# A longer first and a shorter second filler of matmuls at the start of a fused attention and MLP kernel

## The chip, the cores and the metric

The kernel runs on one core of a Trainium2 chip. The metric is device time of one execution in microseconds (us). "Span" is the time from the first to the last instruction in the trace. It is about 1.7 us shorter than the device time here. Every execution has a device time and a span, but only one execution of each kernel and label left a full trace.

Time before the change: 265.46 us, the median of three executions (265.42 to 265.71).

## The reference, cut to what matters

```python
# x: 1 x 2048 x 640, bf16
g = sigmoid((x * gate_w).sum(-1))          # gate per token
a = linear_attention(x, wqkv) @ wo         # 32 heads of 20; phi(t) = where(t>0, t+1, exp(t)) + 1e-6
b = mixer_and_mlp(x, w1, w2, w3, w4)       # layernorm, gelu, shifted groups, residual, MLP
out = g * a + (1 - g) * b
```

The argument is about the first eight microseconds, in which x tiles 0 to 3 (128 tokens each) are loaded, transposed on TensorE, and multiplied by the q part of `wqkv`.

## The kernel before

A small scheduler in the kernel's Python orders all work and adds the semaphore waits. The order of TensorE's start is this (cuts marked):

```python
sch.dma("act", junk[...], A_wqkv[...], "touch")
dma_in(x_tok[:, 0:2, :], x2[0:256, :]..., "x01")      # x tiles 0 and 1
load_wq(0)
dma_in(x_tok[:, 2:4, :], x2[256:512, :]..., "x23")    # x tiles 2 and 3
for k in range(1, KD):
    load_wq(k)
...
memset(pool, ones_c[:], 1.0)                          # 128 x 768, the fillers' operand
...
NWARM = 5
NWARM2 = 2

def t_x(t):                                           # transpose x tile t on TensorE
    b = bank()
    tr_group(b, [x_tok[:, t, 128 * k:128 * (k + 1)] for k in range(KD)])
    ...
    if t % 2:
        activation(dst, src, ACTF.Copy)               # odd tiles: ScalarE copies PSUM to xT
    else:
        copy(dve, dst, src)                           # even tiles: VectorE
...
def warmup(n, cyc):
    b = bank()

    def fn(e):
        ins = None
        for _ in range(n):
            ins = e.matmul(ps[:, b, :], ones_c[:, 0:128], ones_c[:, 128:640], start=True, stop=True)
        return ins
    pe(fn, [ones_c[:, 0:640]], [ps[:, b, :]], cost=n * cyc)
...
def q_four():
    order = [(0, 0), (1, 0), (2, None), (3, None), (0, 1), (1, 1), (2, 0), ...]   # (tile, k); None: transpose the tile
    stream(order, wq, 128, lambda t, b: phi(b, pq_tok[:, t, :]))
...
addA(("warm",), 0.0, lambda: warmup(NWARM, 427.0))    # first filler
for i in range(2):
    addA(("tx", i), 0.28, lambda i=i: t_x(i))         # transposes of x tiles 0 and 1
addA(("warm", 1), 0.0, lambda: warmup(NWARM2, 300.0)) # second filler
addA(("q", 3), 5.44, q_four)
```

The fillers' results are never read. They exist only to keep TensorE active while nothing real can run.

Of the kernel before, what the change touches and what calls it, by code (L numbers as in the profile page):

```python
# [424 lines left out]
def _build(nc, A_x, A_wqkv, A_wo, B_w1, B_w2, B_w3, B_w4, gate_w, out, dbg=None, stop=None):  # L425
# [42 lines left out]
    ps = nc.alloc_psum_tensor("ps", [128, 8, 512], F32)  # L468
# [5 lines left out]
    ones_c = pa.alloc("ones_c", [128, 768], BF16)  # L474
# [45 lines left out]
    def bank():  # L520
        best = None
        for k_ in range(nbanks[0]):
            b = (bank_rr[0] + k_) % nbanks[0]
            if b in bank_pend or b in bank_hold:
                continue
            lk = sch.locks.get(b)
            tfree = 0.0 if lk is None else sch.ev_time.get((lk[1].sem, lk[1].val), 1e18)
            if best is None or tfree < best[0]:
                best = (tfree, b)
        bank_rr[0] = best[1] + 1  # L530
        bank_pend.add(best[1])
        return best[1]
# [58 lines left out]
    def pe(fn, reads, writes, cost=500.0):  # L591
        for w_ in writes:
            sp_, rl = sch.rects(w_)
            if sp_ == "ps":
                for (_p0, _p1, lo, hi) in rl:
                    for b in range(lo // PS_BANK, (hi - 1) // PS_BANK + 1):
                        bank_pend.discard(b)
        return sch.op("pe", fn, reads, writes, cost=cost)
# [141 lines left out]
        assert tags.get((buf, sl)) == what, ("stale ring slot", buf, sl, what, tags.get((buf, sl)))  # L740

    IT = _Items()
    NWARM = 5
    NWARM2 = 2

    def t_x(t):
        b = bank()
        tr_group(b, [x_tok[:, t, 128 * k:128 * (k + 1)] for k in range(KD)])
        src = psb(b, 0, D).rearrange("p (k c) -> p k c", k=KD)
        dst = xT[:, :, 128 * t:128 * (t + 1)]  # L750
        if t % 2:
            activation(dst, src, ACTF.Copy)
        else:
            copy(dve, dst, src)
# [70 lines left out]
        tag_chk("xn", sx, (which, t))  # L825
        sch.dma("sp", xnT[:, :, 128 * t:128 * (t + 1)], xn[:, sx, :], "trn%d" % slot("trn", 4), transpose=True)

    def warmup(n, cyc):
        b = bank()

        def fn(e):
            ins = None
            for _ in range(n):
                ins = e.matmul(ps[:, b, :], ones_c[:, 0:128], ones_c[:, 128:640], start=True, stop=True)  # L834
            return ins
        pe(fn, [ones_c[:, 0:640]], [ps[:, b, :]], cost=n * cyc)

    def q_tile(t):
        tok = slice(128 * t, 128 * (t + 1))
# [37 lines left out]
    def addA(name, dur, fn, deps=()):  # L877
        IT.add("A", name, dur, fn, deps)

    addA(("warm",), 0.0, lambda: warmup(NWARM, 427.0))  # L880
    for i in range(2):
        addA(("tx", i), 0.28, lambda i=i: t_x(i))
    addA(("warm", 1), 0.0, lambda: warmup(NWARM2, 300.0))
    addA(("q", 3), 5.44, q_four)
    addA(("k", 0), 1.36, k_first)
    for i in range(1, 4):
# [324 lines left out]
def bass_gated_mix__linear_attn_block__mixer_s_mlp__prompt_kernel(  # L1211
    nc, A_x, A_wqkv, A_wo, B_x, B_w1, B_w2, B_w3, B_w4, gate_w, out
):
    assert tuple(A_x.shape) == (1, S, D) and tuple(out.shape) == (1, S, D)
    assert tuple(A_wqkv.shape) == (D, 3 * D) and tuple(A_wo.shape) == (D, D)
    assert tuple(B_w1.shape) == (D, D) and tuple(B_w2.shape) == (D, D)
    assert tuple(B_w3.shape) == (D, F) and tuple(B_w4.shape) == (F, D) and tuple(gate_w.shape) == (D,)
    _build(nc, A_x, A_wqkv, A_wo, B_w1, B_w2, B_w3, B_w4, gate_w, out)
# [28 lines left out]
```

## Time and profile before

| what | value |
|---|---|
| device time, median of 3 | 265.46 us |
| span of the profiled execution (its own device time was 266.33 us) | 264.6 us |
| TensorE (PE) busy | 258.2 us, 98% |
| PE's share of the chain that ended last | 96% |

The head of the page, and the first line of its chain, of the kernel before:

```profile
span 264.6 us, 4264 instructions
PE 258.2 (98%) x1675; PEld 136.4 (52%) x1707; DVE 145.9 (55%) x242; ACT 107.6 (41%) x216; POOL 91.1 (34%) x148
...
PE 96%; DMA 1%; issue 1%; ACT 0%; DVE 0%
```

PE is TensorE, PEld its weight loads, DVE VectorE, ACT ScalarE and POOL GpSimd. TensorE bounds the kernel. A saving at its start should therefore reach the end. The next fence is PE's timeline of the kernel before. The columns are start (us), time from the start of the first to the end of the last instruction of the row (us), engine, line, operation, output and inputs, and a count. In brackets stands the idle time in front and what ended it.

```profile
start us, us, engine line op out<-in xcount [idle before <-releaser]
1.59 2.32 PE L834 MATMUL ps<-ones_c 128*128 128x512 bf16 x5 [1.59 <-POOL ones_c L665]
4.12 1.25 PE L617 MATMUL ps<-ident,x_tok 128*128 128x128 bf16 x10 [0.21 <-DMA x_tok<-in_A_x_dram]
5.16 1.06 PE L834 MATMUL ps<-ones_c 128*128 128x512 bf16 x2
6.01 0.63 PE L858 MATMUL ps<-wq,xT 128*128 128x512 bf16 x1
6.44 0.31 PE L859 MATMUL ps<-wq,xT 128*128 128x128 bf16 x1
...
7.08 1.02 PE L617 MATMUL ps<-ident,x_tok 128*128 128x128 bf16 x10
7.93 0.38 PE L858 MATMUL ps<-wq,xT 128*128 128x512 bf16 x1
```

Read the distances between starts, not the durations, because a duration (0.63 us at 6.01) runs on past the start of the next matmul (6.44). At 6.01 to 6.44 us a 512-column matmul takes 0.43 us. Later in the trace it takes 0.22 us. The first fillers stream until about 1.59 + 5 x 0.427 = 3.73 us. The transposes begin at 4.12 us, so nothing streams for about 0.39 us (the page counts 0.21 us, since the duration that it gives the last filler ends later).

The row at 7.93 us is the first q step after the second group of transposes, and it is called **the first pair**.

### The profile page before, as it was taken

Reading aid. Unit: us, or ns where it says so; the run is one execution under the profiler, and the core shown is the slowest. Engines: PE = TensorE matmul, PEld = TensorE weight load, DVE = VectorE, ACT = ScalarE, POOL = GpSimd, SP = SyncE. Lnnn points to the kernel's source line nnn. Section 1 sums busy time; section 2 is a strip of 40 time slices with the busy share of each in tenths; the row PEclk is TensorE's granted clock in tenths of the full one; section 3 lists DMA queues with packets and bytes.
Section 4 is the critical chain, followed back from the end, with each engine's and each line's share of the span. In section 5 each row is a group of like instructions: output and inputs, shape, how many; then the busy total and the mean of one; then the engine's idle time right before and its main releaser. Section 6 shows DMA issues by size and latency. Waiting matters only on the chain.

```text
span 264.6 us, 4264 instructions
## 1 busy us (share of the span) xinstructions
PE 258.2 (98%) x1675; PEld 136.4 (52%) x1707; DVE 145.9 (55%) x242; ACT 107.6 (41%) x216; POOL 91.1 (34%) x148
## 2 busy tenths in 40 slices
PE   7999999999999999999999999999999999999996
PEld 3655555555555454554444545554545455545553
DVE  0397877899903797999786886312212121122242
ACT  3486767742365758675661031212211222121000
POOL 4003996849774017487821104001110011021020
DMA  6775898551666895253666731120000200002011
GB/s 203 244 103 147 205 146 149 162 115 24 102 121 104 299 373 82 54 99 60 69 124 124 110 68 25 33 93 0 2 0 0 102 0 0 2 0 99 2 50 50
DMA packets 50595, 24.77 MB, mean 94 GB/s; under 512 B 41996, under 2 KB 49165, under 8 KB 50576
## 3 DMA queue, kind: packets, MB, share of 16 engines
q1 hardware_dynamic: 49328, 21.23, 36.3%
q0 software_dynamic: 1152, 3.28, 5.4%
q8 instruction: 13, 0.21, 0.3%
q14 instruction: 6, 0.05, 0.1%
q10 hardware_dynamic: 96, 0.00, 0.0%
HBM read 12.05 MB, written 2.62 MB: 55 GB/s over the span
## 4 chain that ended last, share of the span: by engine, by line
PE 96%; DMA 1%; issue 1%; ACT 0%; DVE 0%
PE ps L606 60%; PE ps L1103 21%; PE ps L786 8%; PE ps L858 2%; DMA x_tok<-in_A_x_dram 1%; PE ps L1085 1%; PE ps L1025 1%; PE ps L617 1%; PE ps L859 1%; PE ps L944 1%; DVE x_tok L645 0%; PE ps L834 0%; ACT h2T L662 0%; ACT M_sb L662 0%
## 5 line engine op out<-in xcount | busy, mean ns | idle before, releaser
L662 ACT ACTIVATE h2T<-ps 128x512 bf16<-128x512 f32 x52 | 31.0, 597 | 86.5 <-PE ps L606 86.5
L606 PE MATMUL ps<-xnT,w_58 128*128 128x512 bf16 x250 | 59.0, 379 | 0.5
L1103 PE MATMUL ps<-w_84,h2T 128*128 128x128 bf16 (+1 forms) x412 | 58.2, 298 | 0.4 <-issue 0.3
L628 POOL TENSOR_SCALAR abx<-x_tok,stg 128x640 f32<-128x640 bf16 x16 | 13.9, 874 | 107.6 <-DVE x_tok L645 71.0
L1103 PEld LDWEIGHTS ps<-w_84,h2T 128*128 128x128 bf16 x416 | 32.4, 98 | 27.8 <-issue 2.1
L645 DVE SCALAR_TENSOR_TENSOR x_tok<-ps,stg,abx 128x640 bf16<-128x640 f32 (+2 forms) x17 | 14.3, 844 | 50.7 <-PE ps L1103 50.7
L606 PEld LDWEIGHTS ps<-xnT,w_58 128*128 128x128 bf16 x260 | 24.3, 98 | 24.9 <-issue 0.4
L645 DVE SCALAR_TENSOR_TENSOR abx<-ps,stg,abx 128x640 f32<-128x640 f32 x16 | 14.1, 882 | 28.5 <-PE ps L606 25.5
L662 ACT ACTIVATE Er<-ps 128x640 bf16<-128x640 f32 x32 | 22.4, 704 | 12.7 <-PE ps L606 8.5
L662 ACT ACTIVATE hsT<-ps 128x512 bf16<-128x512 f32 (+1 forms) x32 | 18.9, 593 | 14.6 <-PE ps L606 14.3
L661 ACT ACTIVATE junk<-x_tok 128x640 bf16<-128x640 bf16 x32 | 23.6, 736 | 2.0 <-DVE x_tok L643 1.7
L606 PE MATMUL ps<-M_sb,pqnT 128*128 128x128 bf16 (+1 forms) x157 | 23.7, 298 | 0.2
L606 PE MATMUL ps<-w_60,hsT 128*128 128x128 bf16 (+1 forms) x158 | 23.6, 298 | 0.1
L786 PE MATMUL ps<-pk_tok,x_tok 128*128 128x128 bf16 (+1 forms) x156 | 23.3, 297 | 0.2
L606 PE MATMUL ps<-xnT,w_59 128*128 128x512 bf16 x96 | 23.2, 379 | 0.3 <-issue 0.2
L606 PE MATMUL ps<-wkg,xT 128*128 128x131 bf16 (+1 forms) x148 | 22.4, 298 | 0.1
L606 PEld LDWEIGHTS ps<-M_sb,pqnT 128*128 128x128 bf16 x160 | 13.3, 98 | 12.4 <-issue 0.4
L606 PEld LDWEIGHTS ps<-w_60,hsT 128*128 128x128 bf16 x160 | 13.3, 98 | 12.2
L628 POOL TENSOR_SCALAR xn<-x_tok,st_54 128x640 bf16<-128x640 bf16 x16 | 17.4, 1090 | 4.7 <-DMA xnT<-xn 4.6
L606 PE MATMUL ps<-wq,xT 128*128 128x128 bf16 (+1 forms) x118 | 18.2, 298 | 0.1
L628 POOL TENSOR_SCALAR xn<-x_tok,st_55 128x640 bf16<-128x640 bf16 x16 | 16.3, 1028 | 3.6 <-DMA xnT<-xn 3.2
L628 DVE TENSOR_SCALAR Er<-Er 128x640 bf16<-128x640 bf16 x32 | 12.0, 375 | 9.4 <-ACT Er L662 9.2
(74 smaller groups left out, 264.2 us busy)
## 6 DMA issues: line engine op xcount, KB each, us to landing
w_58<-in_B_w_dram SPq DMA_DIRECT2D x1, 2160.0 KB, 8.2
w_84<-in_B_w_dram SPq DMA_DIRECT2D x1, 2080.0 KB, 13.6
x_tok<-in_A_x_dram SPq DMA_DIRECT2D x3, 640.0 KB, 5.5
out_dram<-x_tok SPq DMA_DIRECT2D x3, 640.0 KB, 3.3
wq<-in_A_wqkv_dram SPq DMA_DIRECT2D x5, 160.0 KB, 4.4
wkg<-in_A_wqkv_dram SPq DMA_DIRECT2D x5, 160.0 KB, 4.4
wv<-in_A_wqkv_dram POOLq DMA_DIRECT2D x1, 800.0 KB, 6.3
wo_aug<-in_A_wo_dram POOLq DMA_DIRECT2D x5, 150.0 KB, 5.1
```

The source lines that it names most:

```text
L606: ins = e.matmul(out_ap, l, r, start=(i == 0), stop=(i == n - 1))
L617: ins = e.transpose(o, s_, ident[:])
L628: return engf(lambda e: e.tensor_scalar(out_ap, in_ap, s1, s2, op0, op1), rd, [out_ap], cost=cost)
L645: return dve(lambda e: e.scalar_tensor_tensor(out_ap, in0, scalar, in1, op0, op1), rd, [out_ap], cost=cost)
L661: return act(lambda e: e.activation(out_ap, in_ap, func, bias=bias, scale=scale, accum_out=accum), rd, wr, cost=cost)
L662: return act(lambda e: e.activation(out_ap, in_ap, func, bias=bias, scale=scale), rd, wr, cost=cost)
L786: ins = e.matmul(o, l, r, start=(t0 + q_ == 0), stop=(t0 + q_ == NT - 1))
L858: e.matmul(ps[:, b, 0:512], l, w[:, k, 0:512], start=(k == 0), stop=(k == KD - 1))
L859: return e.matmul(ps[:, b + 1, 0:n2], l, w[:, k, 512:512 + n2], start=(k == 0), stop=(k == KD - 1))
L944: ins = e.matmul(o, l, r_, start=st_, stop=sp_, skip_group_check=True)
L1025: ins = e.matmul(o, l, r, start=st, stop=sp)
L1103: ins = e.matmul(o, l, r, start=False, stop=(i == KFF - 1))
```

## The change

The intent is that TensorE be busy without a break from its first instruction until x tiles 0 and 1 land, so that its clock rises earlier. The first filler goes from 5 x 512 to 6 x 512 columns. The second goes from 2 x 512 to 512 + 2 x 128.

```diff
-    NWARM = 5
-    NWARM2 = 2
+    WARM = 3072
+    WARM2 = 768
...
-    def warmup(n, cyc):
+    def warmup(cols, cyc):
         b = bank()
+        steps = [512] * (cols // 512) + [128] * (cols % 512 // 128)
 
         def fn(e):
             ins = None
-            for _ in range(n):
-                ins = e.matmul(ps[:, b, :], ones_c[:, 0:128], ones_c[:, 128:640], start=True, stop=True)
+            for n in steps:
+                ins = e.matmul(ps[:, b, 0:n], ones_c[:, 0:128], ones_c[:, 128:128 + n], start=True, stop=True)
             return ins
-        pe(fn, [ones_c[:, 0:640]], [ps[:, b, :]], cost=n * cyc)
+        pe(fn, [ones_c[:, 0:640]], [ps[:, b, :]], cost=cols * cyc)
...
-    addA(("warm",), 0.0, lambda: warmup(NWARM, 427.0))
+    addA(("warm",), 0.0, lambda: warmup(WARM, 0.834))
...
-    addA(("warm", 1), 0.0, lambda: warmup(NWARM2, 300.0))
+    addA(("warm", 1), 0.0, lambda: warmup(WARM2, 0.42))
```

## The prediction

> **What bounds the kernel now.** TensorE. The page has PE busy 258.2 of 264.6 us (98%), and the chain of waits that ended last is PE for 96% of the span, DMA for 1% and issue for 1%. After 8 us the view of waits shows no single PE wait over 0.2 us. So a microsecond saved on TensorE at the start should reach the end, unless a later load or VectorE/ScalarE has too little slack.
>
> **What happens at the start (timeline of PE).** The five 512-column fillers begin at 1.59 us, 0.43 us apart, so their streaming is over near 3.73. The transposes of x tiles 0 and 1 begin at 4.12, when the x load issued at 0.80 us has landed (3.27 us in the chain). That leaves about 0.39 us without streaming. Everything up to 7.08 us is slow: 512-column matmuls 427 ns apart, transposes 107 ns apart; from 7.93 us on a 512 plus 128 pair takes 0.27 us, half. The ten transposes from 7.08 to 7.93 fit some six slow and four fast ones, so the clock rises at about 7.7 us: 3.6 us after the break, 6.1 us after the first matmul. The profile's granted clock reads 1.00 throughout, so only the spacing shows this. [...]
>
> **What the change does.** It adds a sixth 512 filler: streaming then ends near 1.59 + 6 x 0.427 = 4.15 us, so the transposes start at most 0.03 us later. The second filler shrinks from 1024 to 768 columns: 0.64 us slow or 0.33 fast instead of 0.85. No other work is added or moved; the emission order should stay nearly the same, since most scheduling dependences shift with TensorE.
>
> **Costing.** [...] transposes to about 5.2, filler to 5.6, first q step to 5.85. The second q step then waits for ScalarE's copy of tile 1 (0.70 us, about 5.4 to 6.1): a new PE idle near 0.3 us. It ends near 6.4, when x tiles 2 and 3 land (issued 1.82 us, 4.6 us to landing), so their transposes run about 6.4 to 6.95 instead of ending at 7.93. The wq slices (issued from 2.3 us on, about 4.5 us each) land just before use. Gain: 0.95 us. If the clock still rises at 7.7 us, only the shorter filler counts: 0.2 - 0.03 = about 0.15 us. Nearly all of either lies on the critical path. I weigh the first case more[...].
>
> **Predicted:** 264.7 us (0.3% faster), range 264.2 to 265.5. Chances: faster by over 2% 0.01, within 2% 0.98, slower by over 2% 0.01.
>
> **What would show it right.** PE timeline: six fillers, no gap before the transposes at about 4.15; spacing halved near 5.1 us rather than 7.7; the first pair after the second transposes near 7.0 instead of 7.93; a short idle before the second q step released by ScalarE's copy; everything after it shifted by the same 0.9 us, and the same idle total later.
>
> **What would make it wrong.** [...] X tiles 2 and 3 or a wq slice may land too late to be used sooner, so that PE waits for DMA instead. A different instruction order later, or a fixed-time load, may take the shift back.

The costing began from a rise of the clock near 5.1 us, an assumption, and its times from "transposes to about 5.2" on hold for that rise. The sum came to a gain of 0.95 us with this rise and of about 0.15 us with the rise still at 7.7 us. Weighed together they gave 264.7 us, 0.76 us under the 265.46.

## The result, and the profile after

In the first set of runs the changed kernel took 265.70 us, the median of 6 executions (264.97 to 266.20). The kernel before took 265.65 us in the same rounds (265.42 to 266.42). The ratio is 0.9994, with a 95% interval of 0.9974 to 1.0015: the same. A ratio here is the mean time of one kernel's fast executions over that of the other's of the same rounds, so it is not quite the ratio of the medians.

The two profiled executions look quite different from that verdict. The head of the page, its chain, and PE's timeline of the changed kernel:

```profile
span 263.2 us, 4300 instructions
PE 259.0 (98%) x1709; PEld 135.5 (51%) x1709; DVE 145.4 (55%) x242; ACT 107.7 (41%) x216; POOL 91.0 (35%) x148
...
PE 98%; DVE 0%; POOL 0%; issue 0%; POOLq 0%
```

```profile
1.58 2.74 PE L835 MATMUL ps<-ones_c 128*128 128x512 bf16 x6 [1.58 <-POOL ones_c L665]
4.17 0.76 PE L617 MATMUL ps<-ident,x_tok 128*128 128x128 bf16 x10
4.77 0.49 PE L835 MATMUL ps<-ones_c 128*128 128x512 bf16 x3
5.33 0.38 PE L859 MATMUL ps<-wq,xT 128*128 128x512 bf16 x1
5.54 0.22 PE L860 MATMUL ps<-wq,xT 128*128 128x128 bf16 x1
...
6.01 0.72 PE L617 MATMUL ps<-ident,x_tok 128*128 128x128 bf16 x10
6.57 0.38 PE L859 MATMUL ps<-wq,xT 128*128 128x512 bf16 x1
```

The ten transposes from 4.17 us take 0.60 us to the next row instead of 1.04. The clock has risen by then, and the first pair stands at 6.57 us instead of 7.93, so 1.36 us earlier. All of that arrives at the end. These are the last rows of VectorE's timeline, first of the kernel before, then of the changed one:

```profile
261.32 1.08 DVE L645 SCALAR_TENSOR_TENSOR x_tok<-ps,stg,abx 128x512 bf16<-128x512 f32 x2 [1.92 <-PE ps L1103]
```

```profile
259.96 1.07 DVE L645 SCALAR_TENSOR_TENSOR x_tok<-ps,stg,abx 128x512 bf16<-128x512 f32 x2 [1.92 <-PE ps L1104]
```

The difference is 1.36 us again. The order of instructions on every engine is the same in both traces, apart from the fillers (for TensorE by its weight loads, as some matmul records are missing). So one pair of profiles says "1.36 us faster", and the executions say "no difference". The explanation is in the executions. The six spans of the changed kernel are 263.2, 263.5, 263.8, 264.1, 264.2 and 264.5 us. The profile caught the fastest of them. The profiled execution of the kernel before (266.33 us) was slower than all three timed ones that came with it (265.42 to 265.71). A single profile of each was a draw from two wide distributions that overlap.

The trace's record of the granted clock says what is drawn. It holds only changes of the clock: a start, a duration, and the granted share. For the changed kernel's profiled execution it reads as follows (ns; the span starts at 10414 and ends at 273650 on the same scale):

```
start 14680   duration 259413   share 1.0
start 274093  duration 1603     share 0.5
```

The clock rose at 14680 - 10414 = 4266 ns, so at 4.27 us of the span. It stayed up for 259413 ns. A later trace shows one other duration (256000 ns, with three fillers); the two differ by 3413 ns. Every rise below is read from this record, unless it is said to come from the spacing. The kernel before has no record in its trace, so its rise was read from the spacing: about 7.7 us. The page's granted clock reads 1.00 in both, though the 512-column matmuls before the rise stood 0.43 us apart and those after it 0.22 us. It can't be used for the start.

### The profile page after: what moved, and what is told of

Read it like the earlier page. It is cut to its first block, busy times and chain, and to the rows that moved or that the text cites. A ratio compares the mean times of both kernels' runs of the same rounds, so it can differ in the third digit from the quotient of the medians.

```text
span 263.2 us, 4300 instructions
## 1 busy us (share of the span) xinstructions
PE 259.0 (98%) x1709; PEld 135.5 (51%) x1709; DVE 145.4 (55%) x242; ACT 107.7 (41%) x216; POOL 91.0 (35%) x148
## 4 chain that ended last, share of the span: by engine, by line
PE 98%; DVE 0%; POOL 0%; issue 0%; POOLq 0%
PE ps L606 61%; PE ps L1104 22%; PE ps L786 8%; PE ps L859 2%; PE ps L835 1%; PE ps L1086 1%; PE ps L1026 1%; PE ps L945 1%; PE ps L860 1%; PE ps L617 0%; DVE x_tok L645 0%; POOL ones_c L665 0%; POOLq L1233 0%
## 5 line engine op out<-in xcount | busy, mean ns | idle before, releaser
L606 PE MATMUL ps<-xnT,w 128*128 128x512 bf16 x360 | 84.3, 379 | 0.0
L1104 PE MATMUL ps<-w,h2T 128*128 128x512 bf16 (+1 forms) x416 | 58.7, 299 | 0.0
L606 PEld LDWEIGHTS ps<-xnT,w 128*128 128x128 bf16 x360 | 33.5, 98 | 33.5 <-issue 0.4
L1104 PEld LDWEIGHTS ps<-w,h2T 128*128 128x128 bf16 x416 | 32.4, 98 | 27.8 <-issue 2.1
L628 POOL TENSOR_SCALAR xn<-x_tok,st 128x640 bf16<-128x640 bf16 x32 | 33.5, 1056 | 12.2 <-DMA xnT<-xn 11.8
L606 PE MATMUL ps<-M_sb,pqnT 128*128 128x512 bf16 (+1 forms) x160 | 23.9, 299 | 0.0
L786 PE MATMUL ps<-pk_tok,x_tok 128*128 128x512 bf16 (+1 forms) x160 | 23.9, 299 | 0.0
L606 PE MATMUL ps<-w,hsT 128*128 128x512 bf16 (+1 forms) x160 | 23.7, 299 | 0.0
L606 PE MATMUL ps<-wkg,xT 128*128 128x512 bf16 (+1 forms) x150 | 22.6, 299 | 0.0
L606 PE MATMUL ps<-wq,xT 128*128 128x512 bf16 (+1 forms) x120 | 18.3, 299 | 0.0
```

The costliest lines, as they stand in the source:

```text
L606: ins = e.matmul(out_ap, l, r, start=(i == 0), stop=(i == n - 1))
L628: return engf(lambda e: e.tensor_scalar(out_ap, in_ap, s1, s2, op0, op1), rd, [out_ap], cost=cost)
L786: ins = e.matmul(o, l, r, start=(t0 + q_ == 0), stop=(t0 + q_ == NT - 1))
L1104: ins = e.matmul(o, l, r, start=False, stop=(i == KFF - 1))
```

## The experiments

Two theories were put side by side after the first result.

- **W (a sum).** What counts is how long TensorE streamed in all in the last microseconds before the rise. A break costs only its own length from the sum. When the rise comes differs between executions.
- **U (unbroken work).** The clock rises about 3.6 us after unbroken work began, as it did in the first profile of the kernel before (4.12 to 7.7 us), and the break of 0.39 us sets the count back to zero. This is what the prediction had built on.

Both are conjectures. The ranges of the rise that the expectations give under W are estimates. The earliest rise is the first matmul plus about 2.5 us of streaming, plus the break where there is one (1.58 + 2.5 = 4.1 us for the changed kernel, 4.4 to 4.5 us for the kernel before). With three first fillers or none it is the start of the transposes at 4.12 us plus 2.5 us, so 6.6 us. The 2.5 us lie between 2.31 us, streamed in the kernel before from 1.59 to about 4.29 us without a rise there, and 2.66 us, streamed in the changed kernel from 1.58 us to the rise at 4.27 us. The latest rise is put 3.4 us after the earliest, the size of the 3413 ns above; that this bounds it was not shown.

Four sets of runs were made, each on one chip, with the kernel before run 11 times in each set. Below, "mean" is the mean of one kernel's executions in us.

### The two kernels again, unchanged

The first two runs of set one had no edit.

> The changed kernel again, unchanged. Theory W [...]: the rise falls anywhere from about 4.1 to 7.5 us, so this profile will show another rise than the 4.2 us of the first, and the spans of its executions spread over about 1.2 us or more. Rival U [...]: this profile shows the rise near 5 us or earlier like the first one, and spans agree within 0.3 us. Rival N (the spread comes from somewhere after 20 us, not from the start): the first pair after the second transposes stands at the same time as in the first profile (6.57 us), and the span differs all the same.

Measured: the rise came at 6.55 us and the first pair at 7.29 us. The mean was 265.64 (265.07 to 266.98), and the ratio to the kernel before was 0.9982 (0.9960 to 1.0005). PE's timeline:

```profile
1.58 2.74 PE L835 MATMUL ps<-ones_c 128*128 128x512 bf16 x6 [1.58 <-POOL ones_c L665]
4.15 1.25 PE L617 MATMUL ps<-ident,x_tok 128*128 128x128 bf16 x10
...
7.29 0.38 PE L859 MATMUL ps<-wq,xT 128*128 128x512 bf16 x1
```

> The kernel before again, unchanged. W: the rise falls anywhere from about 4.4 to 7.8 us, most likely earlier than the 7.7 us of the first profile, and the first pair after the second transposes correspondingly earlier than 7.93, by half the difference of the rises. U: the rise is again at 7.5 to 7.8 us and the pair at 7.93. Mean of its spans: as the changed kernel plus 0.1 to 0.3 us by W; plus about 1.3 us by U.

Measured: the rise came at 4.87 us and the first pair at 6.97 us. The mean was 265.79, ratio 0.9991 (0.9973 to 1.0009) to the other executions of the very same kernel. PE's timeline of this copy of the kernel before:

```profile
1.58 2.31 PE L834 MATMUL ps<-ones_c 128*128 128x512 bf16 x5 [1.58 <-POOL ones_c L665]
4.14 1.06 PE L617 MATMUL ps<-ident,x_tok 128*128 128x128 bf16 x10 [0.24 <-DMA x_tok<-in_A_x_dram]
5.04 0.59 PE L834 MATMUL ps<-ones_c 128*128 128x512 bf16 x2
5.53 0.38 PE L858 MATMUL ps<-wq,xT 128*128 128x512 bf16 x1
...
6.97 0.38 PE L858 MATMUL ps<-wq,xT 128*128 128x512 bf16 x1
```

This is the decisive reading against U. The same code, with the same break before 4.14 us, has its clock up 0.73 us after the break. The copy of the changed kernel, with no break, has it up only at 6.55 us. In this pair of profiles the old kernel is the faster one, by 0.32 us at the first pair. The kernel with the earlier rise is the faster one in both pairs, whichever code it runs. The rival N of the expectation (the spread comes from later) falls too. The time from the first pair to the end was 256.66 or 256.67 us in all four of these profiles.

### Fewer first fillers

```diff
-    NWARM = 5
+    NWARM = 3
```

> Three first fillers instead of five in the kernel before: the break before the first transposes grows from 0.39 to about 1.25 us, nothing else moves. W: [...] the rise comes at 6.6 to 10.0 us, on average 2.2 us later than before, and the time grows by about 1.1 us (266.7 us, ratio 1.004). U, and any rule by which the break of 0.39 us already spoils the count: same rise and same time as before, within 0.1%.

Measured: the rise came at 8.36 us. The mean was 266.72, ratio 1.0023 (1.0002 to 1.0044). The break is now an idle of 1.13 us on the page:

```profile
1.58 1.46 PE L834 MATMUL ps<-ones_c 128*128 128x512 bf16 x3 [1.58 <-POOL ones_c L665]
4.17 1.25 PE L617 MATMUL ps<-ident,x_tok 128*128 128x128 bf16 x10 [1.13 <-DMA x_tok<-in_A_x_dram]
...
8.20 0.46 PE L858 MATMUL ps<-wq,xT 128*128 128x512 bf16 x1
```

The direction is W's. U's "same within 0.1%" is not excluded by this run: the interval begins at 1.0002. The size was too large in my expectation: 0.6 us in its own rounds instead of 1.1. I had taken half a microsecond of time for each microsecond of rise. The profiles give less: 4.27 to 6.57 and 6.55 to 7.29 in the changed kernel, so 0.72 / 2.28 = 0.32 us per us. A faster clock is partly spent on waiting at the start, for example 0.27 us for the load of x tiles 2 and 3 in the run without a second filler below. The expected shift of 2.2 us of rise is then worth 0.7 us, an estimate that fits the 0.6 us.

```diff
-    addA(("warm",), 0.0, lambda: warmup(NWARM, 427.0))
+    # first filler left out
```

> No first filler at all in the kernel before. W: [...] the rise comes at 6.6 to 10.0 us as with three fillers: time equal to that run within 0.2%, about 1 us (0.4%) over the kernel before. U: same time as before within 0.1%. A third view, that any filler before the break helps in proportion to its length, would put this run slower than the one with three fillers by as much again as that one is slower than before.

Measured: rise 7.15 us, mean 266.80, ratio 1.0026 (1.0010 to 1.0042). This looks like a hit for W, but the run was flawed. PE waited 0.34 us for ScalarE's copy of x tile 3, which neither theory foresaw. Printing the bank choices of the kernel's Python showed the cause. Leaving the filler out also leaves out its PSUM bank (the kernel deals out eight of them for TensorE's results). All later banks shift, and q tile 2 gets bank 0, from which ScalarE is still copying x tile 3; in the kernel before it gets banks 2 and 3, and tile 3 has bank 1. The same flaw is in the run without a second filler below. This run was therefore repeated with the bank still taken:

```diff
-    addA(("warm",), 0.0, lambda: warmup(NWARM, 427.0))
+    addA(("warm",), 0.0, lambda: bank_pend.discard(bank()))
```

> No first filler in the kernel before, as in the earlier run without one, but its PSUM bank is still taken, so that every later bank is chosen as in the kernel before. The earlier run had moved q tile 2 onto the bank that ScalarE was still copying tile 3 from, a wait of 0.34 us (0.5 us of streaming) that the filler as such does not cause. Now: no such wait, 256.7 us from the first pair after the second transposes to the end if the clock is up by then. W [...]: rise 6.6 to 10.0 us and the time of the run with three fillers, 266.7 us, within 0.25 us; 0.7 us or more over the kernel before. View that the fillers help in proportion to their length: clearly slower than with three. View that the break of 0.39 us spoils the count anyway: as the kernel before.

Measured: five executions of 266.41 to 267.39, mean 266.86, ratio 1.0033 (1.0014 to 1.0052). One further execution took 703.61 us; it is set aside here (see the last section), but it is the one that was traced, so this kernel's rise and the absence of the wait were not seen. Within its noise no first filler costs the same as three, both 0.6 to 0.9 us over the kernel before, while the step from three to five gains all of it. W had expected the same time for both. A gain in proportion to filler length would put no filler at about 1.5 us (2.5 x 0.6, an estimate). The interval here (0.4 to 1.4 us) leaves that just outside, but the one of three fillers is too wide (0.1 to 1.2 us) for the times alone to exclude it. The view that five fillers with a break are already spoilt is excluded, since leaving them out would then cost nothing, and it cost 0.4 to 1.4 us.

### The two halves of the change, alone

```diff
-    WARM2 = 768
+    WARM2 = 1024
```

> The first filler of six matmuls alone; the second filler stays at 1024 columns as before. W [...]: the rise is drawn from the same range as in the changed kernel, about 4.1 to 7.5 us, 0.4 us earlier than before on average; four profiles so far give about 0.33 us of time for one us of rise, so about 0.13 us (0.05%) is gained on the kernel before, inside the noise of 0.2%. At a given rise the first pair after the second transposes stands where it does in the kernel before (line through 4.87, 6.97 and 7.7, 7.93). U (unbroken work needed) is already against the runs; it would give 0.9 us or more.

Measured: rise 4.65 us, mean 265.75, ratio 1.0001 (0.9984 to 1.0019). The timeline of this run shows two things:

```profile
1.58 2.74 PE L835 MATMUL ps<-ones_c 128*128 128x512 bf16 x6 [1.58 <-POOL ones_c L665]
4.49 0.79 PE L617 MATMUL ps<-ident,x_tok 128*128 128x128 bf16 x10 [0.16 <-DMA x_tok<-in_A_x_dram]
...
6.91 0.38 PE L859 MATMUL ps<-wq,xT 128*128 128x512 bf16 x1
```

First, x landed late, so even six fillers left a break. Streaming stopped near 1.58 + 6 x 0.427 = 4.14 us, 0.35 us before the transposes. The aim of the change, no break until x lands, depends on a landing time that moves by 0.3 us between executions (transposes from 4.15 us in the first copy of the changed kernel, from 4.49 us here). Second, the clock rose 0.16 us after that break. U can't produce this. The expected line for the first pair (6.90 us at a rise of 4.65) was met with 6.91.

This execution did not keep its early start. A later wait for a transposing DMA took 0.5 us of it back, as the waits of PE in the same run show (columns: who waited, for whom, total us, times, longest us):

```profile
PE ps L606 <- DMA xT<-x_tok: 0.3, 1, 0.3
```

It stands at 42.28 us in the chain. From the first pair to the end took 257.16 us instead of 256.67. Whether the early start caused this wait was not tested.

```diff
-    WARM = 3072
+    WARM = 2560
```

> The shorter second filler alone (768 columns), the first stays at five matmuls with the break of 0.39 us. W: rise from the range of the kernel before, about 4.4 to 7.8 us; at a given rise the first pair stands up to 0.2 us earlier than in the kernel before if the clock is still low during the second filler, and not earlier where the clock rose before it, since the second q step then waits for the copy of tile 1 anyway. Time 0.1 to 0.2 us less than before, inside the noise.

Measured: rise by spacing about 7.65 us (no record in this trace), first pair at 7.98 us with x landed 0.36 us later than in the first profile of the kernel before. The mean was 265.90, ratio 1.0007 (0.9990 to 1.0024). Neither half shows a gain that the noise lets through.

### A start 0.3 us earlier

```diff
-    WARM = 3072
+    WARM = 3584
...
-    memset(pool, ones_c[:], 1.0)
+    memset(dve, ones_c[:, 0:256], 1.0)
...
-        steps = [512] * (cols // 512) + [128] * (cols % 512 // 128)
+        steps = [128] * (cols // 128)
...
-        pe(fn, [ones_c[:, 0:640]], [ps[:, b, :]], cost=cols * cyc)
+        pe(fn, [ones_c[:, 0:256]], [ps[:, b, 0:128]], cost=cols * cyc)
```

> The changed kernel with the first matmul earlier: only 256 columns of the ones are set, on VectorE, and the first filler is 28 matmuls of 128 columns, from about 1.0 us to about 4.0 us. W: [...] it is drawn from about 3.5 to 6.9 us; at 0.33 us per us of rise the time falls by 0.2 us against the changed kernel, to 265.4 us on average[...]. If the count needed unbroken work up to the rise, the gain would be the same 0.6 us of rise; if the rise hung on something other than TensorE's own activity (a fixed time after launch), nothing would move.

Measured: the first matmul came at 1.25 us, not at 1.0, so only 0.33 us earlier. The rise was at 6.22 us, within the expected 3.5 to 6.9 us. The mean was 265.99, ratio 1.0014 (0.9993 to 1.0035). The expected 0.2 us faster was missed. At the first matmul's real time the expected gain is only 0.1 us, which six executions can't show. The run is inconclusive.

### More copies, a shorter second filler, and a longer first one

> The changed kernel a third time, to narrow the mean and to see one more rise. W [...]: a rise between about 4.1 and 7.5 us, different from 4.27 and 6.55; [...] the stretch from the first pair after the second transposes to the end 256.7 us if PE meets no late load there. Mean of its times 0.1 to 0.3 us under the kernel before. Unbroken work needed: 0.9 us or more under it.

Measured: rise 6.59 us, first pair 7.33 us, 256.67 us from there to the end, full clock for 259413 ns. The mean was 265.65, ratio 1.0001 (0.9989 to 1.0013). The mean gain that I had expected did not show in this set.

```diff
-    addA(("warm", 1), 0.0, lambda: warmup(WARM2, 0.42))
+    # second filler left out
```

> The changed kernel without its second filler. W: less streaming between 5.2 and 6.1 us in executions where the clock is still low, so little change of the rise; there the q steps start 0.2 to 0.3 us earlier, bounded by the copies of tiles 0 and 1 (about 5.4 and 6.1 us). Where the clock rose before the filler nothing changes. Time 0 to 0.15 us under the changed kernel, inside the noise. If every break put the count back to zero, the two breaks that this opens (about 0.2 us each, before the two q steps) would put the rise at 9.5 us or later in nearly every execution and the time at 266.5 us or more.

Measured: rise 4.79 us, mean 266.06 of 5, ratio 1.0017 (1.0005 to 1.0029). The breaks before the two q steps (which start at 5.53 and 5.96 us) came after the rise, so this execution does not test whether a break puts the count back. The waits of PE:

```profile
PE ps L859 <- DVE xT L671: 0.4, 1, 0.4
PE ps L859 <- ACT xT L662: 0.3, 1, 0.3
PE ps L617 <- DMA x_tok<-in_A_x_dram: 0.3, 1, 0.3
```

The second line is the bank flaw described above, so not all of the loss is the filler's. The third line is not a flaw. Chain of the same run:

```profile
1.82 4.81 DMA x_tok<-in_A_x_dram
6.63 0.05 issue
6.68 0.75 PE ps L617 x10
```

The load of x tiles 2 and 3 landed only at 6.63 us. With an early rise TensorE arrives before it and waits. In the first profile of the changed kernel it had landed before 6.01 us. So an early rise can't always be used.

```diff
-    WARM2 = 768
+    WARM2 = 128
```

> The changed kernel with a second filler of one 128-column matmul, which keeps all PSUM banks as they are (the run without this filler moved them, with the same wait of 0.34 us before q tile 2). W: no such wait; rise from the range of the changed kernel; time 0 to 0.15 us under the changed kernel, so 265.5 to 265.7 us, faster than the kernel before by at most 0.15%. If the second filler is needed to keep the count: rise at 9.5 us or later and 266.4 us or more.

Against the expectation, the banks are not all those of the changed kernel: the kernel's Python now gives tile 3 bank 3 and q tile 2 banks 0 and 1. But q tile 2 no longer gets the bank that ScalarE copies from. Measured: no wait for that copy, only 0.17 us before the second q step for ScalarE's copy of tile 1; rise 5.71 us; mean 265.95, ratio 1.0002 (0.9981 to 1.0023). No gain over either kernel is shown.

```profile
4.18 1.25 PE L617 MATMUL ps<-ident,x_tok 128*128 128x128 bf16 x10
5.21 0.32 PE L835 MATMUL ps<-ones_c 128*128 128x128 bf16 x1
5.57 0.43 PE L859 MATMUL ps<-wq,xT 128*128 128x512 bf16 x1
```

The short filler streams until about 5.21 + 0.11 = 5.32 us, so 0.24 us are empty before 5.57, and the clock rose 0.14 us after this break. The view that the second filler is needed to keep the count falls: the expectation had put the rise at 9.5 us or later for it, and it came at 5.71 us.

```diff
-    WARM = 3072
+    WARM = 3584
```

> Seven first fillers instead of six in the changed kernel, so that no break is left even where x lands 0.3 us late. W: the rise stays in the range of the changed kernel [...]; the transposes start at about 4.57 us when the clock is still low there, 0.4 us later than with x landed at 4.15 and 0.1 us later than with x landed at 4.48; time 0.2 to 0.3 us over the changed kernel. If breaks mattered, this kernel would be the first that always has none, and would be faster than both.

Measured: rise 6.67 us, transposes from 4.55 us, first pair 7.57 us, mean 265.96 of 5, ratio 1.0013 (1.0001 to 1.0025). This is 0.3 us over the changed kernel of the same rounds, as W expected, though with 0.4 us of noise either way on this difference it is not shown. The kernel that had no break in its trace is not the fastest. It only starts the transposes later.

### All rises together

Streaming is counted from first starts and spacings, in the 3.413 us that ended at the rise and in the 3.413 us before that. The length is the 3413 ns by which the two durations of full clock differ. A stretch that reaches back before the first matmul has that time as idle.

| profile | rise, us | streaming in the 3.413 us ending there | streaming in the 3.413 us before | first pair, us |
|---|---|---|---|---|
| changed | 4.27 | 78% | 0% | 6.57 |
| changed, copy 1 | 6.55 | 99% | 46% | 7.29 |
| changed, copy 2 | 6.59 | 99% | 47% | 7.33 |
| before, copy | 4.87 | 84%, with the break in it | 0% | 6.97 |
| first filler of six alone | 4.65 | 80%, with a break in it | 0% | 6.91 |
| three fillers | 8.36 | 100% | 60% | 8.20 |
| seven fillers | 6.67 | 100% | 49% | 7.57 |
| no first filler, bank shifted | 7.15 | 80% | 0% | 7.83 |
| start 0.33 us earlier | 6.22 | 100% | 46% | 7.17 (from the next record; its own is missing) |
| no second filler | 4.79 | 94% | 0% | 7.25 |
| short second filler | 5.71 | 92%, with a break in it | 21% | 7.06 |

Every stretch that ended at a rise was streamed for at least 78%, and none of those before it for more than 60%. The two traces without a record add earlier stretches of about 68% (the kernel before) and 62% (the shorter second filler alone), if their rises are taken from the spacing. The transposes are counted as streaming here. If they did not count, the stretch that ended at the rise without a first filler would have 50%, and the earlier ones of the two traces without a record 62%, so the two groups would overlap, if those two rises are read rightly. The longest unbroken stretch alone does not separate them either: the same 2.13 us of five fillers preceded a rise at 4.87 us in the copy of the kernel before and one at 7.7 us in its first profile. Full clock lasted 259413 ns in all of these but one, and 256000 ns in that one (three fillers). What sets the moment of the rise within one kernel (4.27, 6.55 and 6.59 us in the three profiles of the changed one) was not shown.

## Why the prediction was right or wrong

**Right: what bounds the kernel, and that a gain at the start passes to the end.** TensorE stayed at 98% in both profiles, and the 1.36 us between the first pairs came out as 1.36 us at the end. The instruction order stayed the same.

**Right: the class.** "Within 2%" had 0.98, and every set says the same.

**Right: what an early rise brings.** The chain of the estimate (copy of tile 1, tiles 2 and 3, first pair near 7.0 for a rise near 5.1) came close: 6.97 us at a rise of 4.87, and 6.57 at 4.27.

**Wrong: the step that sized the gain.** The prediction took the time from the break to the rise in the one profile ("3.6 us after the break") for the time that the clock needs once work is unbroken. From it came the rise near 5.1 us in the costing and "Gain: 0.95 us". Two things in it failed.

1. The break did not set the rise back. The rise came at 4.87 us, 0.73 us after the break of the kernel before, and at 4.65 us, 0.16 us after a late-x break. What separates the traces is the sum of streaming: at least 78% in the 3.413 us before each rise, at most 60% (or 68%) in the 3.413 us before that. If the sum decides, closing the break moves the rise by its 0.4 us (an estimate from the break of 0.39 us), and not from 7.7 to 5.1 us.
2. One profile's rise was taken for the kernel's. The prediction named a rise that varies by run as a risk but did not carry it through: in the second profile of the kernel before the rise came at 4.87 us, not at 7.7. The kernel before did not have the expected 2.6 us to win on average.

The term of the sum that was mis-sized is the mean shift of the rise: about 2.6 us expected, about 0.4 us by W (the length of the break). At 0.32 us per us this is 0.13 us. The shorter second filler adds at most 0.21 us (256 columns at the low clock) in those executions where the clock is still low there. Both are estimates from the numbers above. Measured over all sets, the changed kernel's mean is 265.64 (18 executions) and that of the kernel before 265.82 (56 executions): 0.19 us less, with a 95% interval of 0.24 us either way from the spread of the executions. That pools chips whose means for the kernel before ran from 265.61 to 266.11. The single ratios are 0.9994, 0.9982 and 1.0001. A gain of 0.95 us is excluded. A gain of 0.1 to 0.3 us is possible and not shown.

**The range.** The stated 264.2 to 265.5 us was laid around the 265.46 of three executions. The median of the 18 is 265.62, just outside it. Against the kernel before in the same rounds (ratio 0.9994 x 265.46 = 265.30) it would lie inside. That is no support for the mechanism: the range reached up to no change at all. The point estimate promised more than came in either case.

**Where the rest of an early rise goes.** Three waits were seen to take part of it back in single executions: the copy of tile 1 (0.17 us before the second q step), the load of tiles 2 and 3 (up to 0.27 us), and a transposing DMA at 42 us (0.3 us on PE, 0.5 us of span). How often each occurs is not known.

**Open.** Two executions lie well above the others of their kernel: 266.98 us for the changed kernel (the next is 266.20) and 267.06 for the early start (266.09). They were not traced. How much streaming a rise needs, what sets its moment, and whether the two halves of the change gain anything, lie below what these runs resolve. No version among the runs beats both kernels.

## What to carry to other kernels

When two kernels differ only in the first microseconds, compare many executions, and ask of each profile when its clock rose before you compare anything else in it. One profile of each showed 1.36 us here, for a change whose mean effect is at most about 0.4 us. Fill idle time at the start: with three first fillers or none instead of five, this kernel took 0.6 to 0.9 us more. But don't pay with real work to close the last short break: with seven, the transposes started at 4.55 us and the time was 0.13% over the kernel before (0.01% to 0.25%). When you remove an instruction for an experiment, keep the buffer rotation as it was, or you measure that instead.

## The one execution of 703.61 us

One of six executions of the kernel with no first filler took 703.61 us instead of 266.9. Its 512-column matmuls took 833 ns on average instead of 379 in the other traces, twenty matmuls of mixed width took 7.43 us instead of 2.73, so 0.37 of the full rate there, and 266.9 / 703.61 = 0.38 over the whole execution. Its clock record was empty (as in two ordinary executions), and ScalarE's 128x512 activations kept their 597 ns. It was seen once, and its cause was not shown. The averages of the groups in that execution:

```profile
L606 PE MATMUL ps<-xnT,w 128*128 128x512 bf16 x360 | 223.1, 833 | 0.0
...
L662 ACT ACTIVATE h2T<-ps 128x512 bf16<-128x512 f32 x52 | 31.1, 597 | 295.6 <-PE ps L606 295.6
```
